# Products of a zero tile from the start of the program, and a new order for the first blocks of a chained linear attention and two gated layers

## The chip, the cores and the metric

One core of one Trainium2 chip runs the program. The metric is the device time of one execution in microseconds (us); lower is better. TensorE is called PE, its weight loads PEld, VectorE DVE, ScalarE ACT, GpSimd POOL; SP issues most DMAs.

## The reference, cut to what matters

Three steps follow each other on 3072 tokens (4 batches of 768), all in float32:

```
y      = chunked linear attention(x, a, B, C)      # 8 heads, state 16 x 32, decay a per token
x1     = (sigmoid(y @ w_gate) * (y @ w_val)) @ w_out          # 256 -> 1536 -> 256
h      = x1 @ w_in
result = (h * sigmoid(h)) @ w2_out                            # 256 -> 2048 -> 256
```

In the attention the decays are multiplied up along the sequence (a scan), M = (C B^T) * L gives the part of y from the same chunk, and a state that is handed from chunk to chunk gives the rest. The kernel uses chunks of 128 tokens, so there are 24 tiles q = 0 to 23, six to a batch.

## The kernel before, in words

**Attention, by tile q.** `at_load_bc`, `at_load_x` and `at_loadL` load B, C, x and the decays; the decay tile L comes to all partitions by a DMA of 512 KB (line 342) from `ac_d`, which `decays` prepares. `at_wide1` transposes B and C on PE (line 368, tiles 0 to 3), ACT writes them as `bT` and, head by head, into `x1T` (lines 373, 379). `at_L` scans L on DVE (line 422). `at_cb` multiplies C with B on PE (line 461) and L by the result on DVE (line 472). `at_y` forms y from the state (line 481) and from L and x (line 488); `at_state` and `at_state2` advance the state (PE line 504, DVE lines 512, 514 and 526). `at_yT` splits y into a high half on ACT (line 541) and a low half on DVE (line 543): `xT`, the input of the first gated layer.

**First layer, by block b and slice f.** Blocks have 2, 2, 4, 4, 4, 4, 4 tiles, so block 0 needs tiles 0 and 1, block 1 tiles 2 and 3. The 1536 hidden columns are 12 slices f. `m1_gate` and `m1_val` multiply in three terms of high and low halves (line 581; the third uses the low half of the weights); `m1_out` adds into `acc` (line 635). Each slice's weights are loaded as three DMAs (lines 290, 290, 295) and converted by `conv` and `conv_r`: ACT line 260, DVE lines 262 and 264, POOL lines 270 and 273, ACT line 275 (high half), DVE line 277 (low half), ACT line 310. Products against the weights of slice f wait for these.

**Second layer.** It follows after the attention and is written in a loop; the change leaves it alone.

**What sets the order.** `ORDER` is a text of names and indices. Each token runs one generator to its next `yield`, and the instructions of all engines are recorded in that order; every engine runs its own in order. `b a x` load, `e` is `decays` (four parts), `t L cb ct y st S yt` are the attention steps above, `l w wr z` load and convert a weight slice, `g v lo o` are the first layer, `l2 w2 wr2` the weights of the second.

**Products of zeros.** `zeros(n)` multiplies a tile of zeros, `zz`, by itself n times into the second half of the PSUM tile `ps_e`, which nothing reads afterwards there (128x512, bfloat16, line 233). Before the change this is done behind the transposes of tile 2 (four times) and of tile 3 (six times), by the table `ZW`.

Of the kernel before, what the change touches and what calls it, by code (L numbers as in the profile page):

```python
# [36 lines left out]
g.0.0 v.0.0 v.0.0 w.2 l.4 g.0.1 cb.2.1 g.0.1 l.4 w.3 l.4 r.4 a.4 z.1 v.0.0 l.5 w.3 cw.3 l.6 t.3 t.3 ct.2
cb.2.1 o.0.0 t.3 x.3 r.4 p.4.1.0 w.3 v.0.1 wr.3 v.0.1 y.2.0 w.2 st.2 w.3 y.2.0 y.2.1 st.2 cb.3.0 v.0.1 t.3
S.2 w.4 bw.3 p.4.1.2 l.5 o.0.0 w.3 yt.2 cb.3.0 l.5 g.0.2 l.6 yt.2 v.0.2 w.4 v.0.2 l.6 w.3 w.4 g.0.2 cb.3.1
b.5 wr.4 w.3 b.5 p.4.0.1 o.0.1 w.4 g.0.2 cb.3.1 g.0.3 ct.3 L.4 w.4 v.0.3 ct.3 g.0.3 y.3.0 g.0.3 st.3 y.3.0  # L40
w.5 y.3.1 o.0.1 v.0.2 l.7 yt.3 st.3 v.0.3 wr.5 o.0.2 yt.3 l.7 v.0.3 l.7 g.1.1 w.5 cw.4 w.4 g.1.0 l.8 p.4.0.2
# [839 lines left out]
```

## Time and profile before

| | us |
|---|---|
| median of 3 runs | 645.76 (645.73 to 645.94) |
| the profiled execution | 644.25 |
| span of its instructions | 642.4 |
| PE busy in the span | 626.6 (98%) |
| DVE, ACT, POOL busy | 419.8, 327.5, 107.6 |

The span runs from the first to the last instruction of the program; the 1.9 us between it and the execution's own time lie around it. The profiled execution is 1.5 us below the median of the runs. Times in the rows count from the start of the span. A matmul of full float32 is recorded as two instructions (x2 for one product), and a few records of PE are missing. In a timeline row stand start, length, engine, line, operation, output<-inputs, shape, count, and in brackets the idle time before it with what ended it.

### The profile page before, as it was taken

To read this page: it belongs to the slowest core of one execution; us is meant where nothing else is said; L and a number is where in the kernel's file an instruction comes from. 1 tells how busy PE (TensorE), PEld (TensorE's weight loads), DVE (VectorE), ACT (ScalarE), POOL (GpSimd) and SP (SyncE) were. 2 spreads that over 40 slices of the span, in tenths; PEclk is the share of its full clock that TensorE was granted. 3 is DMA by queue.
4 is the path that set the end of the run, shared out by engine and by line. 5 is a ranking of instruction groups with operands and counts; after the bars stand their busy time and mean duration, and the time that the engine had idled before them with its cause. 6 is when DMAs were issued, how large, how long until landed. Compare 5 with 4: busy or idle time off the path is not lost.

```text
span 642.4 us, 9844 instructions
## 1 busy us (share of the span) xinstructions
PE 626.6 (98%) x3680; PEld 517.4 (81%) x3682; DVE 419.8 (65%) x660; ACT 327.5 (51%) x649; POOL 107.6 (17%) x129
## 2 busy tenths in 40 slices
PE   5799999999999999999999999999999999999997
PEld 2489998887788778778877878888888888888886
DVE  7989998776865767854358784564655544645644
ACT  5677754444444555344347664554544544544533
POOL 3676513212121223110003210000000000000000
PEclk9999999999999999999999999999999999999999
DMA  9999859736664573511004300000010100100000
GB/s 226 208 250 245 168 138 159 149 59 143 147 139 88 157 141 67 147 49 34 1 6 132 124 2 0 1 34 0 1 35 0 34 0 1 34 0 1 34 0 34
DMA packets 140143, 51.17 MB, mean 80 GB/s; under 512 B 119008, under 2 KB 133536, under 8 KB 140096
## 3 DMA queue, kind: packets, MB, share of 16 engines
q1 hardware_dynamic: 139952, 50.41, 33.4%
q8 instruction: 29, 0.48, 0.3%
q14 instruction: 18, 0.15, 0.1%
q10 hardware_dynamic: 144, 0.13, 0.1%
HBM read 36.80 MB, written 3.24 MB: 62 GB/s over the span
## 4 chain that ended last, share of the span: by engine, by line
PE 86%; DVE 4%; ACT 2%; DMA 1%; issue 1%; POOL 1%; SPq 0%; ACTq 0%; DVEq 0%; POOLq 0%
PE h L581 20%; PE g L581 14%; PE acc L635 13%; PE o L785 13%; PE v L581 13%; PE o L806 7%; PE cb L469 2%; PE y L488 2%; PE y L481 1%; DMA raw<-in_moe_w_out_dram 1%; DVE cvt L264 1%; POOL cvt L273 1%; DVE cvt L262 1%; PE st L504 1%; DVE gl L614 0%
## 5 line engine op out<-in xcount | busy, mean ns | idle before, releaser
L581 PE MATMUL g<-xT,w 128*128 128x512 f32 (+1 forms) x504 | 122.7, 367 | 1.2 <-DVE w L277 0.8
L581 PE MATMUL v<-xT,w 128*128 128x512 f32 (+1 forms) x504 | 120.8, 365 | 0.5 <-ACT sg L595 0.5
L581 PE MATMUL h<-x2T,w2b 128*128 128x512 f32 x432 | 107.0, 389 | 0.0
L760 DVE TENSOR_TENSOR sh<-h,sh 128x512 f32<-128x512 f32 x96 | 66.1, 691 | 61.4 <-ACT sh L759 59.8
L769 DVE TENSOR_TENSOR gl<-sh,gh 128x512 fp32r<-128x512 f32 x96 | 65.8, 690 | 57.2 <-ACT gh L764 55.6
L581 PEld LDWEIGHTS g<-xT,w 128*128 128x128 f32 x504 | 87.4, 188 | 16.7 <-DVE w L277 1.2
L581 PEld LDWEIGHTS v<-xT,w 128*128 128x128 f32 x504 | 86.9, 188 | 15.3 <-ACT sg L595 0.9
L635 PE MATMUL acc<-gh,w 128*128 128x512 f32 (+1 forms) x280 | 99.1, 380 | 0.0
L581 PEld LDWEIGHTS h<-x2T,w2b 128*128 128x128 f32 x432 | 80.7, 188 | 16.5
L759 ACT ACTIVATE sh<-h 128x512 f32<-128x512 f32 x96 | 57.4, 599 | 71.0 <-PE h L581 67.3
L764 ACT CAST gh<-sh 128x512 fp32r<-128x512 f32 x96 | 59.0, 620 | 63.1 <-DVE sh L760 32.0
L604 DVE TENSOR_TENSOR sg<-v,sg 128x512 f32<-128x512 f32 (+1 forms) x84 | 50.8, 610 | 50.2 <-PE v L581 32.1
L785 PE MATMUL o<-w2b,gh 128*128 128x512 f32 x280 | 74.2, 390 | 0.0
L595 ACT ACTIVATE sg<-g 128x512 f32<-128x512 f32 (+1 forms) x84 | 44.5, 535 | 45.3 <-PE g L581 39.5
L573 ACT CAST gh<-sg 128x512 fp32r<-128x512 f32 (+1 forms) x70 | 40.9, 590 | 50.4 <-DVE sg L604 39.4
L273 POOL TENSOR_TENSOR cvt<-cvt,raw 128x512 int32<-128x512 int32 (+1 forms) x28 | 45.3, 1619 | 119.5 <-DVE cvt L264 78.5
L614 DVE TENSOR_TENSOR gl<-sg,gh 128x512 fp32r<-128x512 f32 (+1 forms) x70 | 49.2, 707 | 16.8 <-ACT gh L573 16.5
L785 PEld LDWEIGHTS o<-w2b,gh 128*128 128x128 f32 x280 | 51.8, 188 | 10.3
L635 PEld LDWEIGHTS acc<-gh,w 128*128 128x128 f32 x280 | 52.2, 189 | 9.1 <-issue 0.2
L422 DVE TENSOR_TENSOR_SCAN L<-L,eye 128x1024 f32<-128x1024 f32 x24 | 55.2, 2308 | 0.2 <-POOL L L420 0.2
L635 PE MATMUL acc<-gl,w 128*128 128x512 f32 (+1 forms) x140 | 52.8, 377 | 0.4 <-DVE gl L614 0.2
L472 DVE TENSOR_TENSOR L<-cb,L 128x512 f32<-128x512 f32 x48 | 32.7, 684 | 10.3 <-PE cb L469 10.2
(95 smaller groups left out, 721.1 us busy)
## 6 DMA issues: line engine op xcount, KB each, us to landing
L<-ac_d SPq DMA_DIRECT2D x23, 512.0 KB, 4.8
raw<-in_moe_w_out_dram SPq DMA_DIRECT2D x28, 256.0 KB, 3.9
raw<-in_moe_w_in_dram SPq DMA_DIRECT2D x16, 256.0 KB, 2.6
raw<-in_moe_w_gate_dram SPq DMA_DIRECT2D x12, 256.0 KB, 5.0
raw<-in_moe_w_val_dram SPq DMA_DIRECT2D x12, 256.0 KB, 4.1
x<-in_x_dram SPq DMA_DIRECT2D x24, 128.0 KB, 3.6
out_dram<-o2t SPq DMA_DIRECT2D x20, 128.0 KB, 1.8
bc<-in_B_dram SPq DMA_DIRECT2D x24, 64.0 KB, 3.2
```

What stands on the lines that cost most here:

```text
L273: nc.gpsimd.tensor_tensor(ti, ti, r, ALU.add)
L422: nc.vector.tensor_tensor_scan(t["Lf"], t["Lf"], eye, 0.0, op0=ALU.mult, op1=ALU.add)
L581: nc.tensor.matmul(psum[:, :n], w[:, i, o + k * P : o + (k + 1) * P], xt[j][:, k, :n], start=(z == 0), stop=(z == len(k_terms) - 1),)
L604: nc.vector.tensor_mul(sg[:, :n], ps[:, :n], sg[:, :n])
L614: nc.vector.tensor_sub(lo[:, :n], sg[:, :n], hi[:, :n].bitcast(F32))
L635: mm = nc.tensor.matmul(o, v[:, ms], g[:, :n], start=(f == 0 and z == 0 and not (small and m)), stop=(f == NF1 - 1 and z == len(terms) - 1 ...
L759: nc.scalar.activation(sg, ps, AF.Sigmoid)
L760: nc.vector.tensor_mul(sg, ps, sg)
L764: nc.scalar.copy(hi, sg)
L769: nc.vector.tensor_sub(lo, sg, hi.bitcast(F32))
L785: nc.tensor.matmul(ps, hi[:, s], w2(f)[:, :, DM:], start=(f == 0), stop=False, skip_group_check=True,)
L806: nc.tensor.matmul(ps[:, :DM], g2[b, f][2][:, s], w2(f)[:, 0, DM:], start=False, stop=(f == NF2 - 1), skip_group_check=True,)
```

## The change

Sixteen new tokens `hz.0` to `hz.15`, each one product of zeros, are put into the first 90 or so tokens of `ORDER`: seven behind the transposes of tile 0, nine more up to the first product of tile 0's y. `zz` is set to zero at the very beginning, by DVE instead of POOL. About the first 730 tokens of the table, up to block 2 of the first layer, are rearranged; behind them it is the same but for two tokens. Nothing else is added and nothing is removed. Lines below 202 keep their numbers; later ones move by up to 4 (277 becomes 278, 472 becomes 473, 541 becomes 542).

```
--- before
+++ after
@@
-b.0 e.0 b.0 e.0 l.0 a.0 l.0 l.0 t.0 e.1 b.1 t.0 e.1 e.1 e.2 t.0 cb.0.0 l.1 t.0 e.1 L.0 l.1 e.2 cb.0.1 b.1 L.0
...
+b.0 e.0 b.0 e.0 l.0 a.0 l.0 l.0 t.0 hz.0 e.1 b.1 hz.1 t.0 hz.2 hz.3 hz.4 e.1 hz.5 e.1 e.2 hz.6 t.0 cb.0.0 e.1
+t.0 l.1 L.0 b.1 e.2 hz.7 hz.8 L.0 L.0 cb.0.1 l.1 w.0 l.1 hz.9 x.0 wr.0 a.1 w.0 bw.0 e.2 w.0 t.1 cw.1 a.2
...
+    zz = ap_.tile([P, 512], BF16, name="zz")
+    nc.vector.memset(zz, 0.0)
     warm = wp.tile([P, 96], F32, name="warm")[:, :1]
     nc.vector.memset(warm, 0.0)
...
-    zz = ap_.tile([P, 512], BF16, name="zz")
-    nc.gpsimd.memset(zz, 0.0)
...
+    def heat(i):
+        zeros(1)
+
     def decays(part):
...
-        e=decays, b=at_load_bc, x=at_load_x, a=at_loadL, t=at_wide1, r=at_bc, p=st_part, pt=st_tr, L=at_L,
+        hz=heat, e=decays, b=at_load_bc, x=at_load_x, a=at_loadL, t=at_wide1, r=at_bc, p=st_part, pt=st_tr, L=at_L,
```

Three places show what moves. The first is PE from the start of the program; `bcT0` are the transposes of tile 0, `cb0_0` and `cb0_1` the two halves of its C times B. Before:

```order
L368 MATMUL bcT0_126<-ident_88,bc0_115 128x128 x2
L461 MATMUL cb0_0_141<-x1T_81,bT0_132 128x512
L677 MATMUL ps_e_112<-ident_88,x1T_81 128x32 x6
L461 MATMUL cb0_1_158<-x1T_81,bT0_132 128x512
L368 MATMUL bcT1_178<-ident_88,bc1_130 128x128 x2
L683 MATMUL ps_e_112<-e_i_109,sel_100 128x192
```

And with the change, from the second of the two products of zeros behind the six transposes of the decays:

```order
L234 LDWEIGHTS zz_85
L234 MATMUL ps_e_112<-zz_85 128x512
L462 MATMUL cb0_1_169<-x1T_81,bT0_134 128x512
L234 LDWEIGHTS zz_85
L234 MATMUL ps_e_112<-zz_85 128x512
L369 MATMUL bcT1_186<-ident_90,bc1_131 128x128 x2
L505 MATMUL st0_204<-x0_176,bw0_182 32x64 x4
```

Seven products of zeros stand between `bcT0` and `cb0_0`, two before and one behind `cb0_1`; the product with `sel` moves back behind tile 0's y.

The second place is DVE just ahead of block 0: `cvt7` and `cvt6` are slice 2's weights in conversion, the `w1` row with `cvt4` is the low half of slice 1, the `xT1_0` row the low half of tile 1's y, `dec` the decay of a whole chunk. Before:

```order
L262 TENSOR_SCALAR cvt7_275<-cvt7_275 128x768
L514 SCALAR_TENSOR_TENSOR S2_107<-S2_107,dec_111,st1_277 128x64
L264 SCALAR_TENSOR_TENSOR cvt7_275<-raw5_188,cvt7_275 128x768
L277 TENSOR_TENSOR w1_105<-cvt4_185,w1_105 128x512
L543 TENSOR_TENSOR xT1_0_223<-y1_283,xT0_0_222 128x2x128
L526 TENSOR_TENSOR S1_313<-S2_107,blk_93 128x256
```

With the change:

```order
L263 TENSOR_SCALAR cvt6_265<-cvt6_265 128x768
L265 SCALAR_TENSOR_TENSOR cvt6_265<-raw5_198,cvt6_265 128x768
L544 TENSOR_TENSOR xT1_0_259<-y1_285,xT0_0_258 128x2x128
L278 TENSOR_TENSOR w1_105<-cvt4_196,w1_105 128x512
L697 TENSOR_REDUCE dec_111<-dtmp_110 128x24
L515 SCALAR_TENSOR_TENSOR S2_107<-S2_107,dec_111,st1_307 128x64
L527 TENSOR_TENSOR S1_341<-S2_107,blk_95 128x256
```

The low half of slice 1, the state's step and the reduction of `dec` (before, it stood ahead of the scan of tile 1, with the multiplication `dtmp`) now come behind tile 1's low half.

The third place is ACT ahead of block 1: `xT0_1` is the high half of tile 2's y, the rows with `raw8` are the first step of slice 4's weights. Before:

```order
L379 ACTIVATE x1T_81<-bcT3_372,blk_93 128x128 x4
L260 ACTIVATE cvt12_435<-raw8_346 128x768
L541 CAST xT0_1_443<-y2_407 128x2x128
L275 CAST w1_105<-cvt9_356 128x512
L310 ACTIVATE raw8_346<-raw8_346 128x768
```

With the change:

```order
L276 CAST w1_105<-cvt6_265 128x512
L542 CAST xT0_1_427<-y2_401 128x2x128
L405 COPY st04_430<-bc4_319 128x8x48
L380 ACTIVATE x1T_81<-bcT3_381,blk_95 128x128 x4
L261 ACTIVATE cvt11_451<-raw8_367 128x768
```

The high half of tile 2 now stands ahead of the step that needs slice 4's weights.

## Rows read from the trace of the kernel before

**Rows 1.** Busy time by stretch: stretch, its length, then each engine, clock, DMA.

```profile
3.00:8.30 5.30, 2.87 (x4) 0.87 (x4) 2.56 (x5) 2.35 (x9) 0.56 (x1) 1.00 0.98 267
8.30:17.00 8.70, 7.02 (x39) 3.50 (x38) 8.39 (x12) 5.74 (x13) 3.10 (x5) 1.00 1.08 274
17.00:26.80 9.80, 6.18 (x42) 2.56 (x42) 9.80 (x14) 6.07 (x19) 7.83 (x6) 1.00 1.00 237
42.60:95.00 52.40, 52.25 (x473) 49.08 (x472) 48.22 (x85) 36.83 (x81) 26.60 (x25) 1.00 0.84 190
```

**Rows 2.** Timeline of DVE up to block 1: start, length, instruction, idle before it.

```profile
4.92 0.55 DVE L331 TENSOR_SCALAR x1T<-x1T 32x768 f32<-32x768 f32 x1 [2.10 <-DMA x1T<-in_a_dram]
...
14.41 0.36 DVE L687 TENSOR_TENSOR dtmp<-ps_e,blk 128x192 f32<-128x192 f32 x1
14.80 0.35 DVE L693 TENSOR_REDUCE dec<-dtmp 128x24 f32<-128x192 f32 x1
15.07 0.81 DVE L262 TENSOR_SCALAR cvt<-cvt 128x768 int32<-128x768 int32 x1
...
16.80 2.28 DVE L422 TENSOR_TENSOR_SCAN L<-L,eye 128x1024 f32<-128x1024 f32 x1
...
24.64 0.27 DVE L514 SCALAR_TENSOR_TENSOR S<-S,dec,st 128x64 f32<-128x64 f32 x1
...
25.73 0.68 DVE L277 TENSOR_TENSOR w<-cvt,w 128x512 fp32r<-128x512 f32 x1
26.33 0.41 DVE L543 TENSOR_TENSOR xT<-y,xT 128x256 fp32r<-128x256 f32 x1
...
27.81 2.80 DVE L422 TENSOR_TENSOR_SCAN L<-L,eye 128x1024 f32<-128x1024 f32 x1
...
34.81 0.43 DVE L402 COPY st<-bc 128x256 bf16<-128x256 bf16 x1
...
36.62 0.42 DVE L543 TENSOR_TENSOR xT<-y,xT 128x256 fp32r<-128x256 f32 x1 [0.70 <-ACT xT L541]
...
42.33 0.42 DVE L543 TENSOR_TENSOR xT<-y,xT 128x256 fp32r<-128x256 f32 x1
```

**Rows 3.** Timeline of PE up to block 1.

```profile
6.35 2.07 PE L461 MATMUL cb<-x1T,bT 128*128 128x512 f32 x2 [1.40 <-ACT x1T L379]
...
15.77 1.68 PE L461 MATMUL cb<-x1T,bT 128*128 128x512 f32 x2
...
24.97 0.33 PE L448 MATMUL cwT<-ident,cw 128*128 128x128 f32 x1
25.13 1.02 PE L461 MATMUL cb<-x1T,bT 128*128 128x512 f32 x2
25.99 0.38 PE L581 MATMUL g<-xT,w 128*128 128x256 f32 x1
26.80 1.22 PE L581 MATMUL g<-xT,w 128*128 128x256 f32 x8 [0.42 <-DVE xT L543]
...
30.23 1.24 PE L233 MATMUL ps_e<-zz 128*128 128x512 bf16 x5
...
39.16 0.39 PE L581 MATMUL g<-xT,w 128*128 128x256 f32 x1 [0.65 <-DVE w L277]
...
42.62 0.59 PE L581 MATMUL g<-xT,w 128*128 128x256 f32 x2
```

**Rows 4.** Timeline of SP: issue of the DMAs of the decays of tiles 1 and 2.

```profile
11.02 1.04 SPq L342 DMA_DIRECT2D L<-ac_d  x2
```

**Rows 5.** Tile L, the DMA issued at 11.02 alone: time from issue to landing.

```profile
DMA to landing us min/median/max: 5.4/5.4/5.4
```

**Rows 6.** Chain of waits, 30 to 37 us: start, length, what.

```profile
30.46 4.77 DMA raw<-in_moe_w_out_dram
...
35.41 0.93 ACT cvt L260
```

**Rows 7.** Timeline of POOL under the slow scan.

```profile
26.96 1.49 POOL L273 TENSOR_TENSOR cvt<-cvt,raw 128x512 int32<-128x512 int32 x1
```

More of the change, by code (lines that the diff above doesn't have):

```diff
@@ L37 @@
[L37 to L41, printed above, removed]
@@ L132 @@
[L132 to L133 removed]
+b.0 e.0 b.0 e.0 l.0 a.0 l.0 l.0 t.0 hz.0 e.1 b.1 hz.1 t.0 hz.2 hz.3 hz.4 e.1 hz.5 e.1 e.2 hz.6 t.0 cb.0.0 e.1
+t.0 l.1 L.0 b.1 e.2 hz.7 hz.8 L.0 L.0 cb.0.1 l.1 w.0 l.1 hz.9 x.0 wr.0 a.1 w.0 bw.0 e.2 w.0 t.1 cw.1 a.2
+cb.0.0 w.0 cb.0.1 w.1 l.2 w.0 t.1 w.1 st.0 hz.10 hz.11 w.1 t.1 l.2 w.0 cb.1.0 b.2 L.1 hz.12 t.1 hz.13 l.2
@@ new lines @@
+o.1.0 l.9 w.5 g.0.4 w.6 v.1.3 p.5.1.2 w.7 v.0.4 cw.4 g.0.5 v.1.3 x.6 w.6 v.0.4 cb.4.0 o.1.1 v.0.4 S.3 o.1.0
+w.6 l.10 g.0.5 w.7 o.1.2 g.0.5 l.10 w.7 o.1.2 p.5.1.0 v.0.5 w.6 v.0.5 w.7 o.1.3 v.0.5 w.8 cb.4.0 g.1.5 o.1.1
+p.5.0.1 p.5.0.2 g.0.6 o.0.4 L.5 l.11 g.1.5 g.1.5 g.1.4 x.4 w.7 g.1.4 ct.4 l.10 g.0.6 o.1.3 p.5.1.1 b.6 g.0.6
+cb.4.1 o.0.4 w.8 g.1.4 p.5.0.0 w.8 v.1.4 wr.8 o.0.5 w.7 v.1.4 l.11 wr.9 w.8 v.0.6 pt.5.0 v.1.5 v.1.4 w.9
+v.0.6 v.1.5 v.0.6 o.1.4 v.1.5 pt.5.1 w.9 g.0.7 o.1.4 w.8 w.9 g.0.7 b.6 wr.10 v.0.7 v.0.7 l.11 w.8 o.0.6 w.9
@@ new lines @@
+g.0.7 b.8 g.1.6 v.0.7 g.1.6 cb.4.1 v.0.7 g.0.8 g.1.6 z.0 g.0.8 g.0.8 v.0.8 o.0.5 w.10 a.6 cw.5 g.1.8 lo.0.7
+ct.4 v.0.8 w.10 o.0.6 b.7 r.6 v.0.8 b.7 v.1.6 w.10 v.0.8 r.6 g.1.8 w.9 v.1.6 v.1.8 p.6.1.1 cb.5.0 w.9 w.10
+y.4.0 g.1.8 st.4 y.4.0 v.1.6 y.4.1 w.11 o.1.5 cb.5.0 a.8 v.1.7 p.6.1.0 o.1.6 w.11 wr.11 v.1.8 o.0.7 lo.0.8
+p.6.0.0 v.1.7 p.6.1.2 w.10 w.11 g.1.7 pt.6.1 o.0.8 p.6.0.1 cb.5.1 p.6.0.2 o.1.6 w.10 w.11 pt.6.0 g.1.7 o.1.5
+v.1.8 g.1.7 v.1.7 o.0.8 cb.5.1 o.0.7 b.8 v.1.7 g.0.9 x.5 v.0.9 lo.1.7 r.7 g.0.9 st.4 S.4 g.0.9 g.0.10 r.7
@@ new lines @@
+o.1.10 cb.8.1 pt.9.1 o.1.11 z.1 o.1.11 o.1.11 g.2.3 o.1.11 b.12 v.2.0 v.2.2 b.12 ct.9 lo.2.0 b.11 v.2.2
+lo.2.1 p.10.1.0 y.8.0 y.8.1 g.2.3 z.3 b.11 st.9 L.10 cb.9.0 yt.8 a.11 g.2.2 o.2.0 p.10.1.1 x.12 o.2.0
+p.10.0.0 a.12 v.2.3 v.2.2 bw.10 g.2.5 cw.10 r.10 v.2.3 p.10.1.2 v.2.3 b.13 g.2.5 yt.8 v.2.3 v.2.4 pt.10.1
+v.2.2 lo.2.3 g.2.4 cb.9.0 g.2.5 o.2.1 p.10.0.2 p.10.0.1 S.8 v.2.4 b.13 lo.2.2 r.11 pt.10.0 g.2.4 g.2.4 r.11
+o.2.1 v.2.4 v.2.5 st.9 v.2.5 p.11.1.0 v.2.5 o.2.2 v.2.4 cw.13 v.2.6 cb.9.1 ct.10 cb.9.1 ct.10 cw.11 o.2.3 z.6
@@ new lines @@
+y.9.0 p.11.1.2 L.11 st.10 y.9.0 y.9.1 yt.9 a.13 cb.10.0 p.11.0.1 g.2.6 p.11.0.0 g.2.6 cb.10.0 z.4 g.2.8
+p.11.0.2 S.9 pt.11.0 o.2.2 lo.2.4 v.2.5 st.10 o.2.3 p.11.1.1 lo.2.5 v.2.6 g.2.6 pt.11.1 r.12 S.10 g.2.8 r.12
+cb.10.1 v.2.6 ct.11 b.14 o.2.4 v.2.6 b.14 ct.11 o.2.5 lo.2.6 g.2.8 yt.9 v.2.7 L.12 p.12.1.0 g.2.7 o.2.4 g.2.7
+cb.10.1 g.2.7 bw.12 v.2.7 p.12.0.1 p.12.0.2 p.12.1.2 v.2.7 o.2.5 v.2.7 g.2.9 p.12.0.0 lo.2.7 g.2.9 pt.12.0
+g.2.9 v.2.8 v.2.8 v.2.8 v.2.9 v.2.8 o.2.6 p.12.1.1 v.2.9 p.13.0.0 pt.12.1 r.13 o.2.6 cw.14 cb.11.0 r.13
@@ new lines @@
+y.10.0 cb.11.0 x.11 st.12 y.10.0 p.13.0.2 v.2.9 y.10.1 yt.10 cb.11.1 lo.2.8 p.13.0.1 o.2.7 p.13.1.0 cb.11.1
+v.2.9 g.2.10 st.12 yt.10 p.13.1.1 S.12 g.2.10 lo.2.9 o.2.8 p.13.1.2 L.13 pt.13.1 g.2.11 g.2.11 pt.13.0 g.2.11
+v.2.10 g.2.10 cb.12.0 y.11.0 bw.13 cb.12.0 ct.13 b.16 r.14 y.11.0 y.11.1 a.14 r.14 yt.11 cb.12.1 yt.11 x.13
+v.2.10 v.2.10 p.14.0.1 b.15 o.2.7 v.2.11 v.2.11 v.2.11 o.2.8 p.14.0.2 v.2.11 cb.12.1 g.3.1 ct.13 L.14 v.2.10
+o.2.9 p.14.0.0 g.3.0 p.14.1.1 pt.14.0 p.14.1.0 v.3.0 lo.2.10 g.3.1 b.15 o.2.9 st.13 y.12.0 st.13 y.12.1
@@ new lines @@
+p.16.0.2 v.3.3 o.3.0 p.16.1.2 v.3.3 lo.3.2 g.3.4 pt.16.1 L.15 v.3.5 x.15 o.3.2 x.16 g.3.5 g.3.5 lo.3.3 o.3.1
+bw.15 p.16.0.1 yt.13 v.3.5 v.3.5 g.3.4 g.3.4 o.3.2 p.16.0.0 v.3.4 pt.16.0 g.3.6 v.3.4 b.17 v.3.4 g.3.6 b.18
+L.17 b.18 v.3.6 p.17.0.0 v.3.6 v.3.4 g.3.7 r.17 cb.15.0 y.14.0 cb.15.0 st.15 r.17 p.17.1.1 y.14.0 y.14.1
+v.3.5 p.17.0.2 x.17 cb.15.1 lo.3.4 p.17.0.1 o.3.3 st.15 yt.14 S.15 pt.17.0 r.18 p.17.1.0 o.3.4 g.3.6 cw.17
+o.3.3 v.3.6 p.17.1.2 v.3.7 v.3.6 lo.3.5 pt.17.1 r.18 cb.15.1 o.3.4 bw.16 yt.14 o.3.5 l2.0 l2.0 g.3.7 p.18.0.0
@@ new lines @@
+st.19 v.4.6 o.4.5 lo.4.6 o.4.4 L.21 g.4.7 g.4.8 g.4.8 o.4.5 p.21.1.1 L.22 v.4.8 r.22 g.4.7 g.4.7 v.4.7
+p.21.1.0 p.21.1.2 v.4.7 v.4.7 p.22.0.1 v.4.8 pt.21.1 r.22 v.4.8 v.4.7 w2.3 g.4.10 yt.18 v.4.8 g.4.10 cb.20.0
+w2.3 y.19.0 cb.20.0 ct.20 y.19.0 lo.4.8 y.19.1 p.22.1.1 cb.20.1 lo.4.7 w2.2 r.23 g.4.9 g.4.10 p.22.1.2 yt.19
+v.4.9 p.22.1.0 v.4.9 pt.22.1 g.4.9 g.4.9 x.22 o.4.6 v.4.9 o.4.7 w2.3 v.4.10 p.22.0.2 S.19 r.23 v.4.10 cb.20.1
+cw.22 o.4.6 v.4.9 o.4.7 p.22.0.0 lo.4.9 g.4.11 p.23.1.1 pt.22.0 yt.19 ct.20 v.4.11 p.23.1.2 v.4.10 g.4.11
@@ new lines @@
+w2.2 a.23 v.4.10 v.4.11 g.4.11 lo.4.10 y.20.0 p.23.1.0 st.20 y.20.0 st.20 bw.21 y.20.1 v.4.11 yt.20 cb.21.0
+ct.21 yt.20 ct.21 cw.23 p.23.0.0 o.4.8 cb.21.0 S.20 v.5.0 p.23.0.2 st.21 st.21 cb.21.1 bw.22 y.21.0 pt.23.1
+cb.21.1 ct.22 ct.22 S.21 p.23.0.1 o.4.8 L.23 y.21.0 pt.23.0 y.21.1 st.22 yt.21 cb.22.0 v.4.11 g.5.0 x.23
+st.22 g.5.0 lo.4.11 cb.22.0 v.5.1 yt.21 o.4.9 S.22 cb.22.1 y.22.0 cb.22.1 v.5.0 cb.23.0 y.22.0 cb.23.0 y.22.1
+ct.23 yt.22 ct.23 yt.22 o.4.9 cb.23.1 y.23.0 cb.23.1 v.5.1 y.23.0 y.23.1 yt.23 g.5.0 yt.23 B o.4.10 v.5.0
@@ new lines @@
+l2.4 o.4.11 l2.4 v.5.0 o.4.10 l2.5 lo.5.0 l2.5 g.5.1 g.5.1 g.5.1 g.5.2 v.5.1 o.4.11 o.4.11 v.5.1 g.5.2 o.4.11
+lo.5.1 g.5.3 w2.4 g.5.2 g.5.3 w2.4 w2.4 wr2.4 o.5.0 w2.5 w2.4 v.5.2 wr2.5 w2.5 o.5.1 g.5.3 l2.6 o.5.0 w2.5
+l2.6 v.5.3 w2.5 g.5.4 v.5.2 l2.7 v.5.2 v.5.3 l2.7 v.5.2 o.5.1 lo.5.2 g.5.4 wr2.6 v.5.3 v.5.4 v.5.3 v.5.4
+lo.5.3 o.5.2 wr2.7 o.5.2 g.5.4 g.5.5 v.5.4 g.5.5 v.5.4 v.5.5 g.5.5 lo.5.4 v.5.5 v.5.5 o.5.3 v.5.5 o.5.3
+lo.5.5 g.5.6 g.5.6 g.5.6 v.5.6 v.5.6 v.5.6 o.5.4 v.5.6 o.5.4 lo.5.6 g.5.7 g.5.7 g.5.7 v.5.7 v.5.7 v.5.7 o.5.5
@@ new lines @@
+v.5.7 o.5.5 lo.5.7 g.5.8 g.5.8 g.5.8 o.5.6 v.5.8 v.5.8 v.5.8 o.5.6 v.5.8 g.5.9 lo.5.8 g.5.9 g.5.9 o.5.7 v.5.9
+v.5.9 v.5.9 o.5.7 v.5.9 g.5.10 lo.5.9 g.5.10 g.5.10 o.5.8 v.5.10 v.5.10 v.5.10 o.5.8 v.5.10 g.5.11 w2.5
+lo.5.10 g.5.11 g.5.11 o.5.9 v.5.11 v.5.11 v.5.11 g.6.0 v.5.11 g.6.0 w2.4 o.5.9 g.6.0 w2.4 o.5.10 w2.6 v.6.0
+v.6.0 v.6.0 o.5.10 lo.5.11 v.6.1 g.6.1 g.6.1 g.6.1 v.6.1 v.6.0 v.6.1 g.6.2 lo.6.0 v.6.1 g.6.2 lo.6.1 o.5.11
+w2.5 o.5.11 o.5.11 g.6.2 v.6.2 o.5.11 w2.7 g.6.3 w2.7 v.6.2 w2.6 w2.6 o.6.0 v.6.2 v.6.3 w2.6 v.6.2 o.6.1
@@ L134 @@
+w2.12 g.6.8 w2.11 w2.12 v.6.8 v.6.7 w2.11 g.6.8 g.6.10 w2.12 wr2.12 o.6.6 lo.6.7 w2.12 v.6.8 g.6.10 wr2.13
+o.6.6 v.6.8 l2.14 o.6.7 w2.13 l2.14 g.6.9 w2.12 w2.13 g.6.9 lo.6.8 g.6.9 w2.13 o.6.7 g.6.10 w2.12 v.6.9 w2.13
+v.6.9 v.6.9 o.6.8 w2.13 l2.15 v.6.10 w2.14 l2.15 o.6.8 v.6.9 g.6.11 lo.6.9 v.6.10 w2.13 v.6.10 g.6.11 w2.14
+o.6.9 w2.14 w2.15 v.6.11 wr2.14 w2.15 o.6.9 w2.15 wr2.15 w2.14 v.6.11 g.6.11 w2.15 w2.14 v.6.10 w2.14 w2.15
+lo.6.10 v.6.11 w2.15 v.6.11
 """
```

141 lines of the change are left out of this document (45 added, 96 removed).

## The prediction

> **What bounds the kernel now.** First read the stretches [rows 1]. From 42.6 to 95 us PE is busy 52.25 of 52.40 us: from there on PE is the bound, and the end moves by what its stream of products moves. Before 26.8 us it isn't: it is idle for 2.43, 1.68 and 3.62 us in three stretches, 7.7 in all, while DVE is busy 8.39 of 8.70 and then 9.80 of 9.80 us. So ahead of block 0 the chain runs through DVE, and behind it the DMAs, whose share is 0.98 to 1.08. Then read where the two chains meet, in the timeline of PE [rows 3]: the first product of block 0 starts at 25.99, but the second, which needs the low half of tile 1, only at 26.80, after DVE's row of 26.33 [rows 2]. PE waits once more at 39.16, 0.65 us for the low half of slice 3's weights, and starts block 1 at 42.62, its second product behind DVE's row of 42.33, which ends at 42.75. So three rows of DVE (tile 1's low half, slice 3's, tile 3's) say when PE may go on, and the change is worth what it takes off them.
>
> The early products also run at half rate. C times B of one half tile takes 2.07 us at 6.35 and 1.02 us at 25.13 [rows 3], about 1.2 against 2.4 GHz, though the granted clock reads 1.00 in both stretches [rows 1]; the one at 15.77 (1.68) stands at the change from one to the other, after PE had been busy 7.02 of 8.70 us.
>
> **The change part by part.** *Products of zeros.* Five of them take 1.24 us [rows 3], 0.25 each at the most; sixteen cost 4.0 us at full rate and 8.0 at half. They stand ahead of 26.8, where PE is idle 7.7 us. Seven stand between tile 0's transposes and C times B. If all are at half rate they start at 4.96 and end at 8.5, the product follows instead of at 6.35, its 2.07 us and 0.8 for the transposes of the decays end at 11.4, two more zeros and the second half at 14.5. DVE needs that at 13.8. So this costs 0 if PE reaches its full rate by about 12 us, and 0.7 at half rate; I take 0, because the old program reached it by 17 with less to do. A higher rate there gains nothing either, as DVE waits for no product between 9.2 and 26.3.
>
> *The zero tile on DVE.* Writing 128x512 bfloat16 takes at most what a pass over 128x768 int32 takes, 0.81 us in the row of 15.07 [rows 2], and DVE waits 2.10 us for the decays before its row of 4.92: 0. Without that cover it would cost up to those 0.81.
>
> *DVE up to tile 1's low half.* Ahead of tile 1's scan the multiplication `dtmp` and the reduction go: 15.07 - 14.41 = 0.66 us [rows 2], so DVE is ready at 16.80 - 0.66 = 16.14. But the decays of tile 1 are issued at 11.02 [rows 4] and land 5.4 us later, at 16.4 [rows 5]. On SP the store of the decays moves ahead of one weight load, yet the DMAs carry the same bytes up to there and are full, so I leave the landing at 16.4 and start the scan at 16.45: 0.35 earlier (0 if it lands later, 0.66 if earlier). Behind it `dtmp` comes back (14.80 - 14.41 = 0.39), slice 1's low half goes (26.33 - 25.73 = 0.60), and the state's step goes (0.2 of its 0.27 us, as rows overlap). Sum: -0.35 + 0.39 - 0.60 - 0.2 = -0.76; with the ends of the landing, -0.4 to -1.1. Tile 1's low half starts at 25.6 instead of 26.33, and block 0's second product at 26.0 instead of 26.80. PE is ready for it: tile 2's half product still stands ahead, and the transpose of 24.97 to 25.13 (0.16) moves into block 0.
>
> *DVE up to block 1.* What was taken out comes back behind tile 1: 0.60 + 0.2 + 0.27 (reduction: 15.07 - 14.80) = 1.07. A copy of 0.43 moves out [rows 2]. The wait of 0.70 before tile 2's low half [rows 2] goes: its high half stood on ACT behind the first step of slice 4, which waits until the weights land at 30.46 + 4.77 = 35.23 and takes 0.93 [rows 6]; now it stands ahead. DVE itself then needs slice 4's step, ready at 36.2, about 0.1 us before it is there. Sum at slice 3's low half: -0.76 + 1.07 - 0.43 - 0.70 + 0.1 = -0.72. PE comes there at -0.80 + 0.16 = -0.64, so its wait of 0.65 stays nearly whole (0.57), and it goes on 0.72 earlier. Tile 3's low half is behind the same DVE chain: another -0.2 (the state's step now follows it), so at 41.4 and done by 41.8; PE's second product of block 1 comes at about 42.0. **Block 1 starts 0.7 us earlier.**
>
> *Behind block 1.* PE has 0.15 us of waits left up to 95 [rows 1], so nothing more is to be had than that; I take 0.05, as the slices' conversions stand on DVE in nearly the same places. All that follows moves as it is. Sum: -0.75 us. The profiled execution, 644.25, becomes 643.5; it is 1.5 below the median of the runs, and the same term taken from the median, 645.76, gives **645.0 us**. A measurement of this kernel can tell about 0.2%, 1.3 us, from no change: the forecast is no change that it could tell.
>
> The Trainium skill, "TensorE: Matmul & The Clock Gate", part 1, says that PE's clock stands at half by default and that activity releases it, which is a reason to fill gaps. The rows agree that the early products take twice as long; by the sum above that is worth 0, by the rule, if PE were the path there, the third rival's 4.9 us.
>
> **The rivals.** *1. More of DVE's time goes.* The scan at 27.81 took 2.80 us, those before it 2.28 [rows 2]; under it ran a POOL product of 1.49 us [rows 7]. If the new order pairs them otherwise, 0.52 goes, and if tile 1's decays land as soon as DVE is ready, 0.31 more: 0.75 + 0.83 = 1.58, 644.2 us. Against it: POOL has the same products in that stretch, and the DMAs are full. The Trainium skill, "GPSIMD Engine Reference", section 1, says that GpSimd and VectorE share interfaces to SBUF and contend when VectorE reads two inputs from there; the slow scan agrees, and the rule gives no sign for the new pairing.
>
> *2. The shift is given back.* Weights land no earlier, since the DMAs are the limit; if slices 4 to 8 hold PE at their old times, the end stays at 645.8. For it: DVE is full up to there. Against it: PE's waits there come to 0.15 us.
>
> *3. PE was the path.* If the chain ahead of 17 us hung on PE's rate, half of its 2.87 + 7.02 us busy there goes, 4.9: 640.8. Against it: DVE is busy 96% from 8.3 on.
>
> *4. Slower: the zeros stand in the way.* PE takes its instructions in order. If its rate rises only after block 0 has begun, everything up to tile 1's y runs at half: 14.5 us as above, then 7 zeros (3.5), two transposes twice (1.8), the two halves for tile 1 (4.1), tile 0's y, state and the rest (2), and the old four zeros behind tile 2's transposes (2), which end at 27.9 (the small ones are estimates at twice the length of their shape's later rows). Tile 1's y, its state and half a C times B follow before block 0, 1.7 us as from 24.3 to 25.99 now, so its second product comes at 29.7 instead of 26.80, 2.9 later; DVE meanwhile does the 1.07 us that were put behind tile 1. 645.76 + 2.9 - 1.07 = 647.6. It decides only if PE is still at half rate at about 21 us. Against it: 15.77 shows the rise with fewer products ahead.
>
> **How the numbers follow.** Forecast 0.48, rival 1 0.22, rival 2 0.13, rival 3 0.05, rival 4 0.12. Faster by over 0.2% are rivals 1 and 3, 0.27; within 0.2% the forecast and rival 2, 0.61; slower is rival 4, 0.12. The range reaches below to rival 1 with the landing's whole 0.66 (643.8) and above over rival 2 with the 0.7 us of zeros at half rate (646.5); it leaves out rivals 3 and 4, 0.17.
>
> **What would show it.** Right: tile 1's scan starts at about 16.45 behind a wait for its DMA; block 0's products start near 26.0 without the wait of 0.42; no wait of 0.70 before tile 2's low half; block 1 near 41.9; PE idle before 26 us down by the sixteen products. C times B near 8 us may take 1.0 or 2.1 without a change in the end. Wrong: a wait of DVE for a product ahead of 24 us (rival 4), block 1 before 41.2 (rival 1), or new waits of PE on the weights' low halves between 45 and 80 us (rival 2).

## The result, and the profile after

| | before | after |
|---|---|---|
| median of 5 runs | 645.76 us (645.39 to 646.16) | 649.30 us (648.38 to 650.75) |
| the profiled execution, its span | 644.25, 642.4 | 649.3, 647.6 |

The changed kernel takes 1.0062 times as long, 95% interval 1.0048 to 1.0075: 3.5 us slower, where 0.75 us faster was forecast. The two profiled executions differ by more, 5.2 us of span, because the one of the kernel before lies 1.5 us below its median and the one of the change on its median.

The stretches of the changed kernel, the same as in [rows 1], with the same columns:

```profile
3.00:8.30 5.30, 4.63 (x11) 1.80 (x11) 2.82 (x6) 2.35 (x9) 0.44 (x1) 1.00 1.00 268
8.30:17.00 8.70, 4.82 (x25) 2.18 (x25) 7.06 (x9) 4.65 (x11) 3.73 (x5) 0.84 1.02 276
17.00:26.80 9.80, 9.43 (x66) 4.54 (x65) 9.56 (x13) 6.31 (x17) 6.60 (x6) 0.80 0.86 213
42.60:95.00 52.40, 50.16 (x430) 46.62 (x428) 49.87 (x81) 35.54 (x76) 26.35 (x25) 1.00 0.75 173
```

The last stretch is the one to look at: PE, busy 52.25 us of it before, is busy 50.16 now, while DVE went from 48.22 to 49.87. Ahead of it the timelines say what became of the first part of the prediction. DVE up to block 1, the rows that answer to [rows 2] (lines of the new file stand up to four lines further down):

```profile
17.21 2.29 DVE L423 TENSOR_TENSOR_SCAN L<-L,eye 128x1024 f32<-128x1024 f32 x1 [0.65 <-DMA L<-ac_d]
...
26.07 0.41 DVE L544 TENSOR_TENSOR xT<-y,xT 128x256 fp32r<-128x256 f32 x1
...
27.77 1.46 DVE L527 TENSOR_TENSOR S<-S,blk 128x256 f32<-128x256 f32 x1
...
35.15 0.41 DVE L544 TENSOR_TENSOR xT<-y,xT 128x256 fp32r<-128x256 f32 x1
...
42.55 0.39 DVE L544 TENSOR_TENSOR xT<-y,xT 128x256 fp32r<-128x256 f32 x1
```

PE over the same time, answering to [rows 3]:

```profile
7.37 1.02 PE L462 MATMUL cb<-x1T,bT 128*128 128x512 f32 x2
...
14.75 0.44 PE L505 MATMUL st<-x,bw 128*32 128x64 f32 x8 [3.14 <-DMA x<-in_x_dram]
...
16.21 2.08 PE L462 MATMUL cb<-x1T,bT 128*128 128x512 f32 x2
...
25.91 1.13 PE L582 MATMUL g<-xT,w 128*128 128x256 f32 x3
...
29.89 1.12 PE L462 MATMUL cb<-x1T,bT 128*128 128x512 f32 x2 [0.64 <-DMA bc<-in_C_dram]
...
42.65 1.21 PE L582 MATMUL g<-xT,w 128*128 128x256 f32 x6
```

Tile 1's decays landed later than forecast (the scan waits until 17.21), its low half came at 26.07 instead of 26.33, and block 1 began at 42.65 against 42.62: by then nothing was won and nothing lost. The loss is behind block 1. PE's two long waits there:

```profile
74.31 0.70 PE L636 MATMUL acc<-sg,x1T 128*128 128x256 f32 x2 [1.06 <-DVE sg L605]
...
79.99 0.63 PE L582 MATMUL g<-xT,w 128*128 128x256 f32 x3 [0.99 <-DVE sg L605]
```

DVE at that time: slice 10's third step, slice 9's low half, the value row that PE waits for, and the same once more for slices 11 and 10:

```profile
70.08 1.03 DVE L265 SCALAR_TENSOR_TENSOR cvt<-raw,cvt 128x768 int32<-128x768 int32 x1
71.42 2.50 DVE L278 TENSOR_TENSOR w<-cvt,w 128x768 fp32r<-128x768 f32 x1 [0.31 <-ACT w L276]
73.84 0.41 DVE L605 TENSOR_TENSOR sg<-v,sg 128x256 f32<-128x256 f32 x1
...
75.84 0.95 DVE L265 SCALAR_TENSOR_TENSOR cvt<-raw,cvt 128x768 int32<-128x768 int32 x1
...
77.26 2.34 DVE L278 TENSOR_TENSOR w<-cvt,w 128x768 fp32r<-128x768 f32 x1 [0.33 <-ACT w L276]
79.53 0.74 DVE L605 TENSOR_TENSOR sg<-v,sg 128x256 f32<-128x256 f32 x2
```

And POOL, whose additions for slices 10 and 11 begin as soon as the third steps are done:

```profile
71.24 1.86 POOL L274 TENSOR_TENSOR cvt<-cvt,raw 128x768 int32<-128x768 int32 x1 [0.95 <-DMA L<-ac_d]
...
76.93 1.86 POOL L274 TENSOR_TENSOR cvt<-cvt,raw 128x768 int32<-128x768 int32 x1 [3.83 <-DVE st L403]
```

The same low halves in the kernel before, for slices 9 and 10, where the first stands ahead of slice 10's third step (69.75), which lets POOL go on, and the second begins before POOL does:

```profile
68.54 0.95 DVE L277 TENSOR_TENSOR w<-cvt,w 128x768 fp32r<-128x768 f32 x1
...
69.75 0.95 DVE L264 SCALAR_TENSOR_TENSOR cvt<-raw,cvt 128x768 int32<-128x768 int32 x1
...
74.39 0.95 DVE L277 TENSOR_TENSOR w<-cvt,w 128x768 fp32r<-128x768 f32 x1
```

```profile
70.77 1.93 POOL L273 TENSOR_TENSOR cvt<-cvt,raw 128x768 int32<-128x768 int32 x1 [2.57 <-DVE cvt L264]
...
74.98 2.09 POOL L273 TENSOR_TENSOR cvt<-cvt,raw 128x768 int32<-128x768 int32 x1 [2.28 <-ACT raw L310]
```

Compare ends: POOL is through at 73.10 and at 78.79, the long DVE rows at 73.92 and 79.60, 0.82 and 0.81 later, a little less than the 0.95 that the row takes alone. By these ends the rows did not run slowly; they stood still until POOL had finished, and the profile counts that as busy. The row at 27.77 is the same case: the state of tile 1, 0.42 when nothing is beside it, took 1.46 under POOL's addition for slice 2.

These are not the only rows that came under POOL, and the kernel before had some too. Take as the usual length of a row the one that a quarter of the rows with the same operation and shape stay under, over all the profiles: from 60 to 84 us the rows of DVE run 4.9 us over it in the change and 2.5 us in the kernel before. The two low halves are 2.9 of the 4.9.

Further on, where the order is the same in both kernels, this execution lost another 1.6 us. PE waited for 0.70 us at 168.29 for a DVE row that was again held under POOL; e4, e7, e10 and e11 below have this wait too, with and without zeros, in the old order and the new, so it belongs to no single part of the change. And a weight of the second layer landed later: ACT waited 2.05 us for it (0.46 before), and PE 0.49 for ACT. This wait of ACT is 1.82 to 2.15 us in the five profiled executions with products of zeros and 0.45 to 0.54 in the nine without, and PE loses 0.7 to 1.1 us from 200 to 310 us in the five, 0 to 0.2 in the nine. It goes with the zeros, then; how they bring it about is not shown.

### The profile page after: what moved, and what is told of

Its sections match the earlier page's. It is cut to its first block, busy times and chain, and to the rows that moved or that the text cites. A ratio compares the mean times of both kernels' runs of the same rounds, so it can differ in the third digit from the quotient of the medians.

```text
span 647.6 us, 9872 instructions
## 1 busy us (share of the span) xinstructions
PE 630.9 (97%) x3698; PEld 519.3 (80%) x3698; DVE 423.8 (65%) x661; ACT 327.3 (51%) x649; POOL 107.5 (17%) x128
## 4 chain that ended last, share of the span: by engine, by line
PE 83%; DVE 5%; SPq 3%; DMA 3%; ACT 2%; issue 2%; POOL 1%; DVEq 0%; ACTq 0%; POOLq 0%
PE h L582 20%; PE o L789 13%; PE g L582 12%; PE acc L636 12%; PE v L582 12%; PE o L810 7%; PE y L489 2%; PE cb L470 2%; PE y L482 1%; DMA raw<-in_moe_w_out_dram 1%; SPq L291 1%; DVE w L278 1%; DMA bc<-in_C_dram 1%; POOL cvt L274 1%; DVE cvt L263 1%
## 5 line engine op out<-in xcount | busy, mean ns | idle before, releaser
L582 PE MATMUL v<-xT,w 128*128 128x512 f32 (+1 forms) x504 | 122.3, 365 | 1.0 <-ACT sg L596 1.0
```

The lines of the kernel that those rows point to most:

```text
L582: nc.tensor.matmul(psum[:, :n], w[:, i, o + k * P : o + (k + 1) * P], xt[j][:, k, :n], start=(z == 0), stop=(z == len(k_terms) - 1),)
```

## The experiments

Twelve kernels, each against runs of the kernel before on the same chip. Their order tables have fewer lines, so a row of L278 above is one of L272 or L273 there.

| kernel | median us | against before, with 95% interval |
|---|---|---|
| the change | 649.30 | +0.62% (0.48 to 0.75) |
| e1 new order, no zeros | 647.66 | +0.39% (0.26 to 0.52) |
| e2 old order, with zeros | 646.33 | +0.16% (0.03 to 0.29) |
| e3 change, two low halves later | 649.03 | +0.60% (0.38 to 0.83) |
| e4 before, one low half later | 647.52 | +0.33% (0.19 to 0.47) |
| e5 change, two low halves earlier | 646.15 | +0.15% (0.05 to 0.25) |
| e6 as e5, no zeros | 646.13 | +0.11% (0.00 to 0.23) |
| e7 no zeros, tile 1's state later | 648.32 | +0.50% (0.35 to 0.66) |
| e8 e6 and e7 together | 645.55 | +0.12% (-0.03 to 0.26) |
| e9 new order to block 1, then old, no zeros | 646.23 | +0.12% (0.00 to 0.24) |
| e10 old order to block 1, then new, no zeros | 647.52 | +0.29% (0.19 to 0.40) |
| e11 as e9, with zeros | 646.31 | +0.14% (0.02 to 0.27) |
| e12 before, one copy earlier | 644.62 | -0.13% (-0.28 to 0.02) |

To compare kernels that do the same work in another order, I counted from each profile what PE had lost by a time: that time less the usual length of every product begun until then, products of zeros at nothing (the usual length of a shape is the mean spacing of its products between 30 and 330 us over all the profiles, the longest 15% left out). From each count that of the kernel before is taken off; the table has the differences in us. A few tenths come from the order alone, up to 0.6 in the rows of 42 and 72. By 310 the counts come near to what the profiled executions differ by, and that of the kernel before lay 1.5 us below its median:

```
by us  change  e1    e2    e3    e4    e5    e6    e7    e8    e9    e10   e11   e12
42     +0.08 -0.28 -0.40 +0.70 -0.27 +0.51 -0.46 -0.39 +0.72 +0.64 +0.32 -0.45 +0.10
72     -0.75 -0.39 +0.14 -0.17 +0.28 -0.35 -0.73 -0.71 +0.48 +0.98 -0.18 -0.13 -0.13
82     +2.72 +2.36 +0.73 +2.97 +2.91 +0.95 -0.32 +1.96 +1.95 +1.82 +3.28 +0.21 +0.06
120    +3.28 +2.91 +0.89 +3.52 +2.95 +1.41 +0.17 +2.51 +2.47 +1.86 +3.94 +0.21 +0.05
310    +4.89 +2.81 +1.92 +4.29 +3.77 +2.37 +0.01 +3.64 +2.80 +2.26 +4.84 +1.56 -0.05
```

From 72 to 82 us, the six kernels in which a low half or a copy on DVE stands still under POOL there (the change, e1, e3, e4, e7, e10) lose 2.6 to 3.5 us; the other seven lose 0.2 to 1.5.

**First: the zeros or the order?** e1 takes the sixteen products of zeros out of the changed table:

```diff
-b.0 e.0 b.0 e.0 l.0 a.0 l.0 l.0 t.0 hz.0 e.1 b.1 hz.1 t.0 hz.2 hz.3 hz.4 e.1 hz.5 e.1 e.2 hz.6 t.0 cb.0.0 e.1
+b.0 e.0 b.0 e.0 l.0 a.0 l.0 l.0 t.0 e.1 b.1 t.0 e.1 e.1 e.2 t.0 cb.0.0 e.1
...
```

> The changed kernel without its sixteen products of zeros; everything else in the order of the change. Theory A (the loss is DVE's: in the new order the low halves of slices 9 and 10 run while POOL adds the next slice, take 2.50 and 2.34 us where 0.95 is usual, and PE waits 1.06 and 0.99 us for the value rows behind them): no change against the changed kernel, 648.5 to 650, 0.4 to 0.7% slower than before, with the two long rows still there. Theory B (the zeros stand in PE's way, rival 4 of the prediction): back to about 645 to 646. Theory C (both): 647 to 648.

Measured 647.66, which is theory C, both. The long rows are there. Of PE's waits in this kernel (engine and line, what it waited for, us in total, times, longest), one from 20 to 43 us, and both that there are from 55 to 100:

```profile
PE cb L456 <- DVE L L467: 0.6, 1, 0.6
...
PE acc L630 <- DVE sg L599: 1.1, 1, 1.1
PE g L576 <- DVE sg L599: 1.0, 1, 1.0
```

So both waits behind 70 us come without any zeros. The first line also corrects the view of the changed kernel: the wait at 29.89 is put down to a transfer there, but it is the mask product on DVE, behind the held state row, that ends it.

e2 puts the zeros into the old order, at the matching places:

```diff
-b.0 e.0 b.0 e.0 l.0 a.0 l.0 l.0 t.0 e.1
+b.0 e.0 b.0 e.0 l.0 a.0 l.0 l.0 t.0 hz.0 hz.1 hz.2 hz.3 hz.4 hz.5 hz.6 e.1
...
-e.2 cb.0.1
+e.2 hz.7 hz.8 cb.0.1 hz.9
...
-y.0.0 st.0
+y.0.0 st.0 hz.10 hz.11
...
-cb.1.0
+cb.1.0 hz.12 hz.13 hz.14 hz.15
```

> The other half of the change: the sixteen products of zeros (and the zero tile on DVE) put into the old order at the matching places on PE. Theory A: no change from before, 645.4 to 646.2, C times B near 9 us at 1.02 instead of 2.07. Theory B: the whole loss, 648 to 650. A part between, 646.5 to 647.5, would say that the zeros take PE's time before block 0.

Measured +0.16% (0.03 to 0.29), about 1 us: more than nothing by a hair, and no part of the two long rows. By the count above this execution loses 1.92, and 1.03 of it after 120 us, where the weight of the second layer landed late. C times B on PE in this kernel:

```profile
7.76 1.57 PE L457 MATMUL cb<-x1T,bT 128*128 128x512 f32 x2
...
10.20 1.02 PE L457 MATMUL cb<-x1T,bT 128*128 128x512 f32 x2
...
16.57 2.08 PE L457 MATMUL cb<-x1T,bT 128*128 128x512 f32 x2
```

The zeros do bring PE to its full rate at 10 us, 1.02 instead of 2.07 [rows 3]; it then waits for transfers and for DVE, and by 16.57 it is back at half.

**The first idea of a cure fails.** e3 leaves the low halves under POOL and only lets the rows that PE waits for go ahead:

```diff
-w.9 w.10 y.4.0 g.1.8 st.4 y.4.0 v.1.6 y.4.1 w.11
+w.10 y.4.0 g.1.8 st.4 y.4.0 v.1.6 y.4.1 w.9 w.11
...
-w.10 w.11 pt.6.0 g.1.7 o.1.5 v.1.8 g.1.7 v.1.7 o.0.8 cb.5.1 o.0.7
+w.11 pt.6.0 g.1.7 o.1.5 v.1.8 g.1.7 v.1.7 o.0.8 cb.5.1 w.10 o.0.7
```

> The changed kernel with only the low halves of slices 9 and 10 moved on DVE: slice 9's behind the value row of block 1, slice 6, and slice 10's behind the value rows of block 1, slices 8 and 7, and the second mask product of tile 5. The low halves still meet POOL, but the rows that PE waits for stand ahead of them. Theory A: PE's waits of 1.06 and 0.99 us go, and the time falls by 1.5 to 2.1, to 647.2 to 647.8. Theory B, or any cause ahead of 70 us: unchanged, 649 to 649.5.

Unchanged, 649.03, where theory A had 647.2 to 647.8. DVE, and PE's waits between 55 and 100 us:

```profile
72.02 2.48 DVE L273 TENSOR_TENSOR w<-cvt,w 128x768 fp32r<-128x768 f32 x1
...
79.44 1.32 DVE L273 TENSOR_TENSOR w<-cvt,w 128x768 fp32r<-128x768 f32 x1
```

```profile
PE acc L631 <- DVE gl L610: 0.6, 1, 0.6
PE v L577 <- ACT sg L591: 0.5, 1, 0.5
PE g L577 <- DVE w L273: 0.4, 1, 0.4
```

PE's two waits of 1 us became three of about half as much. DVE is full there, and letting some of its rows go ahead gains nothing. That the time in which it stands still is what counts is a new theory, A2, and this run does not show it: the second row stood still for only 0.37 us here, and the whole time did not fall. The next runs test it.

**The order alone, made and unmade.** e4 moves one token of the kernel before, slice 9's low half, behind slice 10's third step:

```diff
-v.0.7 w.9 g.1.6 p.6.1.1 o.1.5 g.0.8 a.7 lo.0.7 v.0.8 o.0.6 w.10 p.6.0.0
+v.0.7 g.1.6 p.6.1.1 o.1.5 g.0.8 a.7 lo.0.7 v.0.8 o.0.6 w.10 w.9 p.6.0.0
```

> The kernel before with one token moved: the low half of slice 9 stands behind slice 10's third step on DVE, the step that lets POOL's addition start, as in the changed kernel. Theory A: the row grows from 0.95 to about 2.4 us, DVE's rows behind it come 1.5 us later, and the kernel gets 0.5 to 1.5 us slower, 646.3 to 647.3. Theory B: no change, 645.4 to 646.2, since no zero product is added.

Slower as forecast, and by more, 0.33%, some 2.1 us; but by another row than I named. DVE and POOL:

```profile
70.32 0.95 DVE L272 TENSOR_TENSOR w<-cvt,w 128x768 fp32r<-128x768 f32 x1
71.19 2.04 DVE L397 COPY st<-bc 128x256 bf16<-128x256 bf16 x2
...
76.20 2.66 DVE L272 TENSOR_TENSOR w<-cvt,w 128x768 fp32r<-128x768 f32 x1
```

```profile
70.48 2.53 POOL L268 TENSOR_TENSOR cvt<-cvt,raw 128x768 int32<-128x768 int32 x1 [1.74 <-DVE cvt L259]
```

Here the moved row began 0.16 us ahead of POOL, kept its 0.95, and POOL's addition took 2.53 instead of 1.86. The two copies behind it, 0.35 for both in the kernel before, then stood still, and so did slice 10's low half, which had escaped before by starting 0.59 us ahead of POOL. Whoever starts first goes through; the other one waits.

e5 takes the changed kernel, zeros and all, and puts the low halves ahead of the third step that starts POOL:

```diff
-r.6 v.0.8 b.7 v.1.6 w.10 v.0.8 r.6 g.1.8 w.9 v.1.6 v.1.8 p.6.1.1 cb.5.0 w.9 w.10
+r.6 w.9 v.0.8 w.9 b.7 v.1.6 w.10 v.0.8 r.6 g.1.8 v.1.6 v.1.8 p.6.1.1 cb.5.0 w.10
...
-w.10 w.11 g.1.7 pt.6.1 o.0.8 p.6.0.1 cb.5.1 p.6.0.2 o.1.6 w.10 w.11
+w.10 w.10 w.11 g.1.7 pt.6.1 o.0.8 p.6.0.1 cb.5.1 p.6.0.2 o.1.6 w.11
```

> The changed kernel, zeros and all, with the low halves of slices 9 and 10 moved ahead of the DVE row that lets POOL's next addition start (and slice 9's copy on ACT two places up, so that the low half is ready). Putting them later gave nothing: the rows that PE waits for came no sooner, as DVE as a whole was late. Theory A2 (what is lost is DVE's time under POOL's additions, 1.5 and 1.4 us, not the order of its rows): both rows back at about 0.95, DVE some 2.5 us earlier at 80 us, PE's waits of 1.06 and 0.99 gone, and the time down by 1.5 to 2.5, to 646.8 to 647.8. Rival (the weights or the additions themselves are late, and the rows of DVE only fill the time): unchanged, 649 to 649.5.

646.15, better than the 646.8 to 647.8 expected: the loss falls from 0.62 to 0.15%, intervals far apart. DVE and POOL:

```profile
70.49 1.03 DVE L273 TENSOR_TENSOR w<-cvt,w 128x768 fp32r<-128x768 f32 x1
...
72.65 0.67 DVE L468 TENSOR_TENSOR L<-cb,L 128x512 f32<-128x512 f32 x1
...
73.25 1.57 DVE L258 TENSOR_SCALAR cvt<-cvt 128x768 int32<-128x768 int32 x1
...
75.30 0.96 DVE L273 TENSOR_TENSOR w<-cvt,w 128x768 fp32r<-128x768 f32 x1
```

```profile
72.52 1.87 POOL L269 TENSOR_TENSOR cvt<-cvt,raw 128x768 int32<-128x768 int32 x1 [1.81 <-DVE cvt L260]
```

Both low halves have their usual length, and of PE's waits only the 0.6 us for the mask product is left between 26 and 100 us. What now meets POOL is slice 11's shift, 1.57 instead of 0.56, which PE doesn't wait for.

e6 is e5 without the zeros.

> The same two moves in the new order without the sixteen products of zeros. If the two causes are separate, the gains add: 647.7 less 1.5 to 2.5, so 645.2 to 646.2, no longer to be told from before. If the zeros only mattered through the same rows, it equals the kernel with zeros and the moves.

646.13: the zeros make no difference here. By the count of PE's losses the profiled execution stands at that of the kernel before (+0.01 by 310 us); but it was the fastest of its twelve, 644.43.

**Ahead of block 1.** e7 (no zeros) moves the state of tile 1 away from POOL's addition for slice 2:

```diff
-S.1 b.4 ct.2 w.2 z.2 cb.2.0 v.0.0 g.0.0 g.0.1 x.2 v.0.0
+b.4 ct.2 w.2 z.2 cb.2.0 v.0.0 g.0.0 g.0.1 x.2 v.0.0 S.1
```

> The new order without zeros, and only the state of tile 1 (0.42 us without company, 1.46 under POOL's addition for slice 2) moved on DVE behind tile 2's first mask product and block 0's first value row. This is the place where the predicted shift of 0.7 us got lost. Theory: PE's wait of 0.64 us before tile 2's second half goes, and block 1 starts about 0.6 us earlier than 42.6. If the rows between 70 and 82 us decide the end, the time stays at 647.3 to 648; if the start of block 1 does, 647.0.

PE's wait of 0.64 is gone and block 1 starts at 41.88, against 42.28 in e1. The end, 648.32, is above the 647.3 to 648 expected and no better than e1's. e8 is e7 with the low halves earlier as well.

> Both moves, no zeros: the new order with the three rows taken out of POOL's additions. If the sums hold, the 0.6 us ahead of block 1 and the 1.5 to 2.5 behind it add: 644.6 to 645.6 against 645.5 of before, so at best 0.9 us faster than before and about where the prediction stood.

645.55, at the upper end of what was expected and not to be told from before. In its profiled execution block 1 starts at 44.15, since tile 1's low half came at 27.70. That start scatters by execution: with the order of e1 up to there it is 42.28 in e1, 41.81 in e6 and 43.20 in e9; with the zeros 42.65, 43.27, 43.08 and 41.68 in the change, e3, e5 and e11. The means are 42.4 and 42.7, that of the old order (before, e4, e10, e12) is 43.1. The predicted 0.7 us are within that scatter, and these few executions do not settle them.

**Cut at block 1.** e9 follows the changed table, less its zeros, up to the token of block 1's first product, and the old table for all that is then left; e10 is the reverse; e11 is e9 with the zeros. Up to the cut the tables hold nearly the same tokens, 214 and 215 of them. The changed table and e9 at the cut:

```diff
 g.0.3 wr.5 st.3 v.0.3
-g.1.2 w.5 g.1.1 w.4 v.1.1 p.4.0.2
+z.0 z.1 p.4.1.2 g.1.1 w.5 cw.4 w.4 g.1.0
```

> The order is cut where block 1's first product stands. Here the changed order up to there (without zeros) and the old order from there on. Theory A2 (what is lost is lost between 72 and 82 us, by the new order of slices 9 to 11): the shift of 0.4 to 0.7 us that the count of PE's products shows at 54 to 72 us is kept, 644.7 to 645.3, and no low half of a slice takes over 1.5 us behind 65 us. Rival (the new early order leaves transfers or weights late, which is paid behind block 1 in any order): 647 to 648.

> The counterpart: the old order up to block 1's first product, the changed order from there on, no zeros. Theory A2: the whole loss and no shift, 648 to 649, the low halves of slices 9 and 10 at about 2.4 us each and PE's two waits of about 1 us. Rival: 645.4 to 646.

> As the first of these, with the sixteen products of zeros: what the change does ahead of block 1 and nothing else, the part that the prediction worked out. If the zeros cost what they seemed to in the old order (0.9 us in the profile, 0.16% in the comparison), 645.5 to 646.3; if they cost nothing, as between the two kernels with the low halves earlier (646.15 and 646.13), 644.7 to 645.3.

e10 has the loss without anything of the change ahead of block 1 but the zero tile, which DVE still writes: +0.29%, and DVE's rows and PE's waits as in the changed kernel:

```profile
72.00 2.50 DVE L272 TENSOR_TENSOR w<-cvt,w 128x768 fp32r<-128x768 f32 x1 [0.31 <-ACT w L270]
...
77.83 2.35 DVE L272 TENSOR_TENSOR w<-cvt,w 128x768 fp32r<-128x768 f32 x1 [0.32 <-ACT w L270]
```

```profile
PE acc L630 <- DVE sg L599: 1.1, 1, 1.1
PE g L576 <- DVE sg L599: 1.0, 1, 1.0
```

It stayed below the 648 to 649 expected. e9 and e11 are neither the gain expected of theory A2 nor the rival's 647 to 648: +0.12 and +0.14%. The new early order by itself brings nothing; in e11, which began block 1 at 41.68, 0.94 us before the old kernel, the lead on DVE is 0.75 us at tile 3's low half, 0.38 at slice 5's (47.72 against 48.10), 0.27 at 57 us; PE's, by the count, is 0.13 at 72 and gone by 82.

**The other direction.** e12 takes one held row out of the kernel before:

```diff
-v.1.4 w.9 g.0.7
+v.1.4 w.9 p.5.0.2 g.0.7
...
-w.10 p.5.0.2 g.0.8
+w.10 g.0.8
```

> The kernel before with one token moved the other way: the copy of tile 5's third part (1.55 us at 65.89, under POOL's addition of 2.58 us for slice 9; the same copy takes 0.2 alone) put ahead of the DVE row that lets that addition start. Theory A2, in the gaining direction: the copy falls to about 0.3, the value row that follows comes up to 1.3 us earlier, and PE, which shows 0.15 us of waits there, gains little: no change to 0.7 us faster, 644.8 to 645.6. If DVE were the limit there, 1.3 us faster, 644.2; if DVE's rows under POOL cost nothing, no row and no time changes.

```profile
63.41 0.22 DVE L397 COPY st<-bc 128x256 bf16<-128x256 bf16 x1
```

The copy falls from 1.55 to 0.22 us, and DVE spends most of it waiting 0.90 us for PE shortly after. The time, 644.62, is a little under the 644.8 to 645.6 expected; -0.13% is not surely below before. No version here surely beats the kernel before.

## Why the prediction was wrong

- **The step that failed** is the one behind block 1: a cost of 0.05, "as the slices' conversions stand on DVE in nearly the same places". Nearly the same was not enough: e5, which moves those rows back, takes the loss from 0.62 to 0.15%. A low half that moved from ahead of the next slice's third step to behind it came under POOL's addition, which that step starts; twice, with 1.55 and 1.39 us over its usual 0.95. PE's 0.15 us of waits [rows 1] bounded what could be gained there; I took them as if they bounded the loss too. PE waited 1.06 and 0.99 us for the rows behind them. DVE was busy 48.22 of 52.40 us there, and that was the number to weigh: it had 4.18 us left to make up for a delay.
- **Rival 1 had the mechanism and the wrong sign.** It named the scan that was slow beside POOL and let the new pairing only save 0.52. The new order made more pairings instead, the state of tile 1 and the two low halves the costly ones among them. The price of a pairing was also read too low: the row is held until POOL is done, so it is up to the whole of POOL's instruction, not a share of it.
- **DVE up to tile 1's low half** (-0.76): the sign held, 26.07 instead of 26.33. The landing of the decays, left at 16.4, was 17.2, though its transfer was issued earlier than the 11.02 of [rows 4], at 10.55. In e1 the same row stood at 25.70, in e11 at 25.13, so -0.76 lies inside the scatter.
- **Up to block 1** (-0.7): not there, 42.65. The wait of 0.70 before tile 2's low half went, as forecast (35.15 without a wait, 1.47 us earlier). But the state's step, reckoned at 0.2, took 1.46 for its second part under POOL's addition, and PE waited 0.64 for the mask product behind it. Without that (e7) block 1 starts at 41.88, close to the forecast 41.9, in one execution.
- **The zeros at 0**: the prediction took 0, and this stays open. Between e5 and e6, and e11 and e9, no difference; between the change and e1, and e2 and before, 0.2%. That is from 0 to 1.5 us. Where they have a place, it is the late weight of the second layer, far behind the stretch that the sum looked at; but e5 has that wait as well, and e6 not, and their medians agree. The reason that I gave (PE at full rate by about 12 us) holds only to 11: PE then came to rest for 3.14 us until x of tile 0 landed, the granted clock of the two stretches reads 0.84 and 0.80, and C times B at 16.21 took 2.08 again. Read in shorter stretches the granted clock is 0.50, 1.2 GHz, from 14.3 to 20.5 us and 1.00 from 21.0 on. In all five profiled executions with zeros it reads 0.50 to 0.76 on average from 14.3 to 20.5, in none of the others below 1.00 there. So the zeros brought the full rate early, and PE lost it later, where the others were granted it. No run shows a gain from the higher rate: e2 has it at 10 us and is not faster than before.
- **Rival 4**, the slower one, had the sign and not the cause: block 0's second product stood at 26.54, not at 29.7, and e10 is slower without a single zero. **Rival 2**, the shift given back, is what e9 and e11 look like; in the changed kernel something larger covered it. **Rival 3** shows nowhere: C times B ran at the full rate at 7.37 here, and at 10.20 in e2, and no time fell. But PE did not keep that rate up to 17 us, so its whole 4.9 us had no test.
- **The range** counted the landing twice at its lower end: rival 1's 644.2 already has the whole 0.66 in it, so 643.8 was too low. This decides nothing here.

The parts add up only roughly, as far as the intervals can tell. The late order alone costs 0.29% (e10) and the early part with its zeros 0.14% (e11), 0.43 together, where the change costs 0.62 (0.48 to 0.75). e5 shows that most of it hangs on the two low halves; what the rest is, beyond the zeros, wasn't settled.
